# Reordering the output products of a fused attention and spectral-mix kernel, and moving rows of y by engines

## The chip, the cores and the metric

The kernel runs on one core of a Trainium2 chip. The metric is device time in microseconds for one launch. Engines are named as in the profile: PE (TensorE products), PEld (its weight loads), DVE (VectorE), ACT (ScalarE), POOL (GpSimd) and SP (SyncE, which here only issues transfers).

## The reference

Eight batch rows of causal attention with decay (8 heads, 576 positions, 64 channels each) give x, of shape 8 x 576 x 512. Then x is mixed in frequency space and by a channel matrix:

```python
X = np.fft.rfft(x, axis=1)
Xr, Xi = real(X[:, :64]), imag(X[:, :64])
Yr = einsum('bmd,mde->bme', Xr, w_r) - einsum('bmd,mde->bme', Xi, w_i)
Yi = einsum('bmd,mde->bme', Xr, w_i) + einsum('bmd,mde->bme', Xi, w_r)
Y[:, :64] = Yr + 1j * Yi
y = np.fft.irfft(Y, n=576, axis=1)
u = x + y
out = u + np.maximum(u @ w_ch, 0.0)
```

The weights w_r and w_i are 64 modes of 512 x 512 each in f32, 134 MB together. The output has 9.4 MB.

## The kernel before

**The weight stream.** The weights are cut into 64 tiles. POOL issues their transfers (line 90), which turn f32 into bf16, into a ring of nine buffers with the tag "wb". `emit_modes(n)` multiplies tile n (line 147), and the last half of the tiles (32 to 63) are the second half of the channels, two modes each. DVE adds the result to what the first half left, and writes rows of y's spectrum, "YT", of 2 x modes (line 164). Attention runs beside the first part of this stream.

**z in place of u @ w_ch.** The kernel computes z = u @ w_ch as a second sum with the same shape as u. XW = x @ w_ch is made early (`emit_xw`, line 775), and the rows of y are kept in two forms: t = 0 the rows themselves, t = 1 the rows times w_ch. Both are written into `yy`. Then u and z are each an x part (a product with the identity) plus a y part (a product with the inverse basis, BIe or BIl), and the output is u + max(z, 0).

**Early, mid and late rows.** Half of the modes (YTe) are ready early. `emit_part` adds their y parts into x_all and XW (the "early sums", 36; lines 739, 809 and 810). With four calls of `emit_y` for the early rows themselves they make a list of 40, which a counter spreads over the tiles 48 to 62. The other modes come in two quarters. The mid quarter is made by `emit_mid` (lines 784 to 790), the late quarter needs the last tile, 63, and is made by `emit_late` (lines 843 to 852). `y_rows` (line 723) makes both forms for four batch rows at a time: products with w_ch into `plw` (line 726), transposes into `ply` (line 734). ACT and DVE copy the two results to a buffer `yl`, and `move_rows` (line 704) brings each 32-row piece to its place in `yy` by a transfer: the mid ones on SP, 16 in all, the late ones on POOL. For the first batch row the late pieces are written by ACT and DVE directly (lines 848 and 849).

**The output loop.** There are 20 jobs, five for each pair of batch rows: four of 256 output rows and one of 64 rows of each of the two. The list of types gives jobs 5 and 11 to ACT and POOL (relu at line 887, sum at line 888); the others go to DVE. `emit_x` puts the x parts of a job into two PSUM tiles, pu and pz, and `emit_out` adds the y parts, has ACT copy pu to SBUF (line 883), DVE form the output (line 890), and SP store it (line 900 for 256 rows, line 896 for the half jobs). All PSUM tiles of this stage (pu, pz, A of tile 63, pl of `emit_late`) share one tag with four buffers of two banks each. For job 0 the x parts are issued three times before tile 63.

All these products are 64 x 64 tiles of the array. `pieces` gives the halves: with t = 0 for u and t = 1 for z, a piece's row half is `(b + t + (k if sb == 4 else 0)) % 2`, its column half is k.

**Who sets the order.** The framework's planner orders the instructions of each engine by program order and by its own estimate of when each is ready, so the queue of an engine can differ from the program. `tc.keep_in_program_order` pins an instruction in its place. SP and POOL issue transfers in their queue's order.

Of the kernel before, what the change touches and what calls it, by code (L numbers as in the profile page):

```python
# [21 lines left out]
def kernel(  # L22
# [11 lines left out]
    nc = tc.nc  # L34
# [84 lines left out]
    def emit_modes(n):  # L119
        dc, g = tile_of(n)  # L120
        wb = wtiles.pop(n)
        nm = MG if n < NTH else M2
        if late["psM"] is None:
            z = late["psZ"].tile([128, 2, D], F32, tag="z", name="A")
            A = z[:, 0, 0 : NDC * nm * 2 * B].rearrange(
                "p (e m c) -> p e m c", e=NDC, m=nm
            )
        else:
            A = late["psM"].tile([128, NDC, nm, 2 * B], F32, tag="A", name="A")
        if n < NTH:  # L130
# [12 lines left out]
        for mi in range(nm):  # L143
            m = g * nm + mi
            for eb in range(NDC):
                for i, (w_of, x_of) in enumerate(terms):
                    nc.tensor.matmul(  # L147
                        A[:, eb, mi, :],
                        lhsT=w_of(mi, eb * 128),
                        rhs=x_of(m),  # L150
                        start=(i == 0),
                        stop=(i == len(terms) - 1),
                    )
# [534 lines left out]
    with ExitStack() as bctx:  # L688
# [12 lines left out]
        yy = bsb.tile([128, 2, B // 2, 2, D], BF16, name="yy")  # L701
        yls = [bsb.tile([128, 2, D], BF16, name=f"yl{i}") for i in range(2)]

        def move_rows(yl, i, q, skip, dma):
            for j in range(skip, 4):
                for t in range(2):
                    p0 = HM * ((j + t) % 2) + H2 * i
                    dma(
                        yy[p0 : p0 + H2, 1, 2 * q + j // 2, t, :],
                        yl[H2 * j : H2 * j + H2, t, :],  # L710
                    )

        yflat = yy[:, :, :, :, :].rearrange("p l b t e -> p (l b t e)")
        xTs = [
# [8 lines left out]
        def y_rows(yt, b0, ply, plw):  # L723
            cols = lambda eb: _strided(yt[:, eb, b0, 0:1], [[1, 128]])
            for eb in range(NDC):
                nc.tensor.matmul(
                    plw,
                    lhsT=cols(eb),
                    rhs=wch[:, eb, :],
                    start=(eb == 0),  # L730
                    stop=(eb == NDC - 1),
                )
            for eb in range(NDC):
                nc.tensor.transpose(
                    ply[:, eb * 128 : (eb + 1) * 128], cols(eb), ident_bf[:, :]
                )

        def add(p, lhsT, rhs, first):
# [4 lines left out]
        with ExitStack() as cctx:  # L743
# [40 lines left out]
            def emit_mid(q):  # L784
                pyw = psBig.tile([128, D], F32, tag="big", name="pyw")
                yp = psBig.tile([128, D], BF16, tag="big", name="yp")
                y_rows(YT2[:, 0], 4 * q, yp[:, :], pyw[:, :])
                nc.scalar.copy(yls[q][:, 1, :], pyw[:, :])
                nc.vector.tensor_copy(yls[q][:, 0, :], yp[:, :])
                move_rows(yls[q], 0, q, 0, nc.sync.dma_start)  # L790

            def emit_part(b, sb):
                pA = psBig.tile([128, D], F32, tag="big", name="pA")
# [24 lines left out]
            while nmode < NT - 1:  # L818
# [5 lines left out]
                    nx += 1  # L824
                if nmode > NT - GL:
                    assert nx == B
                    while done < min(len(parts), (nmode - NT + GL) * len(parts) // (GL - 2)):
                        a, sb = parts[done]
                        emit_y(a) if sb is None else emit_part(a, sb)
                        done += 1  # L830
                if 0 <= nmode - NT + GL // 2 - 1 < 2:
                    emit_mid(nmode - NT + GL // 2 - 1)
            assert done == len(parts)

        psZ = bctx.enter_context(
            tc.tile_pool(
                name="psZ", bufs=4, space=bass.MemoryType.PSUM, reuse_waits="tile"
            )
        )
        late["psM"], late["psZ"] = None, psZ  # L840


        def emit_late(q):
            pl = psZ.tile([128, 2, D], F32, tag="z", name="pl")
            ply, plw = pl[:, 1, 0 : D // 2].bitcast(BF16), pl[:, 0, :]
            y_rows(YT2[:, 1], 4 * q, ply, plw)
            if q == 0:
                nc.scalar.copy(yy[HM + H2 : 128, 1, 0, 1, :], plw[0:H2, :])
                nc.vector.tensor_copy(yy[H2:HM, 1, 0, 0, :], ply[0:H2, :])
            nc.vector.tensor_copy(yls[q][:, 0, :], ply)  # L850
            nc.scalar.copy(yls[q][:, 1, :], plw)
            move_rows(yls[q], 1, q, 1 - q, nc.gpsimd.dma_start)

        def pieces(job):
            b, sb, nb, _ = job
# [8 lines left out]
                            BIl[HS[half], c0 : c0 + HM]  # L864
                        )

        def emit_x(job, times=1):
            pu = psZ.tile([128, 2, D], F32, tag="z", name="pu")
            pz = psZ.tile([128, 2, D], F32, tag="z", name="pz")
            for _ in range(times):  # L870
                for t, i, o, hs, src, _ in pieces(job):
                    add((pu, pz)[t][o, i, :], ident_bf[hs, hs], src, True)
            return pu, pz

        def emit_out(job, ps, last):
            b, sb, nb, ty = job
            for t, i, o, hs, _, basis in pieces(job):
                add(ps[t][o, i, :], basis, yy[hs, 1, b // 2, t, :], False)
            pu, pz = (p[:, 0:nb, :] for p in ps)
            uo = wpool.tile([128, 2, 2, D], F32, tag="wb", name="uo")  # L880
            u_sb, o_sb = uo[:, 0, 0:nb, :], uo[:, 1, 0:nb, :]
            if ty != "D":
                nc.scalar.copy(u_sb, pu)  # L883
            if ty == "D":
                nc.vector.scalar_tensor_tensor(o_sb, pz, 0.0, pu, ALU.max, ALU.add)
            elif ty == "Q":
                nc.scalar.activation(o_sb, pz, ACT.Relu)
                nc.gpsimd.tensor_tensor(o_sb, o_sb, u_sb, ALU.add)
            else:
# [30 lines left out]
_INS = ['q', 'k', 'v', 'f', 'moe_w_r', 'moe_w_i', 'moe_w_ch']  # L920
_OUTS = [((8, 576, 512), 'float32')]
# [25 lines left out]
```

## Time and profile before

| | |
|---|---|
| median of 5 runs | 446.21 us (444.36 to 447.98) |
| profiled execution | 445.05 us, span 443.2 us |
| mean granted PE clock | 0.861 |
| busy share of the span | PE 82%, DVE 58%, ACT 51%, POOL 30% |
| DMA | 98.20 MB written, mean 222 GB/s; HBM read 163.73 MB |
| mid moves `yy<-yl` on SP | 16 x 32 KB, issued 373.4 to 384.0 us, 5.2 us to landing |
| late moves `yy<-yl` on POOL | 14 x 32 KB, issued 406.8 to 415.6 us, 2.3 us to landing |
| stores of 512 KB | 16, 3.3 us to landing |

Times are microseconds from the start of the span. A row of a group or of the timeline gives engine, line, operation, the tile written and the tiles read, shapes and count; what stands in brackets is the idle time of the engine before it and what ended it. The share of DMA is the mean over 16 engines. Line 739 is a helper that issues the products of the early sums and of the output loop, so these are told apart by their tiles (pA, pB against pu, pz). The ends of products are modelled: a new group of products started every 0.2 us can show 0.38 us for each.

### The profile page before, as it was taken

What the parts mean: (1) busy time and instruction counts of PE and PEld (TensorE: products, weight loads), DVE (VectorE), ACT (ScalarE), POOL (GpSimd) and SP (SyncE); (2) the same over time, 40 slices, a digit from 0 to 9 for tenths busy, and PEclk for the clock granted to TensorE, in tenths of its full rate; (3) what the DMA queues carried; (4) which work ended last, traced back from release to release, by engine and by line L of the source; (5) the groups of instructions that cost most, each with busy time, mean ns of one, the idle gap of its engine ahead of it and who ended that gap; (6) DMA issues with size and microseconds to landing.
All of it is one profiled execution on the core that took longest, in us unless ns stands there. A gap on an engine that the chain in (4) does not pass through costs nothing.

```text
span 443.2 us, 12213 instructions
## 1 busy us (share of the span) xinstructions
PE 361.9 (82%) x5251; PEld 245.9 (55%) x5269; DVE 257.7 (58%) x643; ACT 223.8 (51%) x336; POOL 134.1 (30%) x204
## 2 busy tenths in 40 slices
PE   2787799999887976877877886999999779887873
PEld 1454566776666665655655665666655435543331
DVE  5687778876565655665656676334325535443554
ACT  3688377774645436436446382243354323333663
POOL 7333332252323323233232211432322323102520
PEclk9997699997977757758669597799999988989998
DMA  8999999999999999999999999999999999991787
GB/s 184 231 235 251 223 235 238 233 221 222 236 212 235 238 209 236 210 238 236 210 237 211 211 212 217 215 211 212 211 211 211 211 211 211 224 189 35 268 328 287
DMA packets 51126, 98.20 MB, mean 222 GB/s; under 512 B 3808, under 2 KB 13280, under 8 KB 51072
## 3 DMA queue, kind: packets, MB, share of 16 engines
q0 software_dynamic: 46688, 86.39, 99.4%
q1 hardware_dynamic: 4304, 10.90, 7.0%
q8 instruction: 41, 0.67, 0.5%
q10 hardware_dynamic: 80, 0.13, 0.1%
q14 instruction: 13, 0.11, 0.1%
HBM read 163.73 MB, written 9.44 MB: 391 GB/s over the span
## 4 chain that ended last, share of the span: by engine, by line
PE 31%; DMA 30%; ACT 13%; DVE 8%; issue 5%; POOL 1%; ACTq 0%; DVEq 0%
DMA wb<-in_moe_w_i_dram 30%; ACT E L517 8%; PE pav L555 7%; PE ps L510 6%; PE A L147 6%; PE tp L458 5%; PE px L598 2%; DVE QTs L473 2%; PE vp L482 2%; ACT KT L471 2%; ACT uo L883 2%; PE pz L739 2%; DVE uo L890 2%; PE px L623 1%; DVE E L532 1%
## 5 line engine op out<-in xcount | busy, mean ns | idle before, releaser
L517 ACT ACTIVATE E<-ps 128x1024 bf16<-128x1024 f32 (+1 forms) x128 | 101.5, 854 | 24.1 <-PE ps L510 14.8
L147 PE MATMUL A<-XT,wb 128*128 128x16 bf16 x2048 | 73.0, 181 | 14.8 <-DMA wb<-in_moe_w_i_dram 9.9
L90 POOL DMA_DIRECT2D wb<-in_moe_w_r_dram x65 | 43.2, 665 | 133.8 <-PE A L147 35.8
L147 PEld LDWEIGHTS <-wb 128*128 128x128 bf16 x2048 | 65.8, 99 | 30.0 <-issue 13.0
L510 PE MATMUL ps<-QTs,KT 64*128 64x64 bf16 (+4 forms) x384 | 56.1, 316 | 17.9 <-ACT E L517 16.7
L90 POOL DMA_DIRECT2D wb<-in_moe_w_i_dram x65 | 43.1, 662 | 78.9 <-DMA wb<-in_moe_w_i_dram 38.8
L555 PE MATMUL pav<-va,E 128*128 128x65 bf16 (+1 forms) x1088 | 53.6, 206 | 4.4 <-DVE x_all L577 3.8
L555 PEld LDWEIGHTS <-E 128*128 128x128 bf16 (+1 forms) x1088 | 43.9, 112 | 20.2 <-issue 9.5
L532 DVE TENSOR_TENSOR E<-E,trimask 128x256 bf16<-128x256 bf16 (+2 forms) x128 | 37.2, 302 | 20.0 <-ACT E L517 19.6
L810 ACT CAST XW<-pB 128x512 bf16<-128x512 f32 x36 | 21.1, 586 | 38.2 <-PE pB L739 38.2
L475 ACT COPY VT<-tp 128x640 bf16<-128x640 bf16 (+1 forms) x32 | 23.2, 755 | 32.9 <-PE tp L458 32.8
L775 ACT CAST XW<-pxw 128x512 bf16<-128x512 f32 x36 | 20.6, 587 | 35.9 <-PE pxw L768 27.4
L510 PEld LDWEIGHTS <-KT 64*128 64x128 bf16 x384 | 19.0, 98 | 30.1 <-issue 20.7
L809 DVE CAST x_all<-pA 128x512 bf16<-128x512 f32 x36 | 24.9, 692 | 18.0 <-PE pA L739 15.6
L768 PE MATMUL pxw<-wch,yy 128*128 128x512 bf16 x133 | 33.8, 387 | 1.0 <-issue 0.3
L471 ACT COPY KT<-tp 128x640 bf16<-128x640 bf16 (+1 forms) x32 | 22.1, 755 | 22.5 <-PE tp L458 22.5
L473 DVE COPY QTs<-tp 128x640 bf16<-128x640 bf16 (+1 forms) x32 | 23.2, 768 | 14.0 <-PE tp L458 13.9
L577 DVE TENSOR_TENSOR x_all<-pav,rcp 128x384 bf16<-128x384 f32 x64 | 29.1, 455 | 0.8
L739 PEld LDWEIGHTS <-ident_bf 64*64 64x64 bf16 (+1 forms) x304 | 15.1, 112 | 23.6 <-issue 18.2
L890 DVE SCALAR_TENSOR_TENSOR uo<-pz,uo 128x1024 f32<-128x1024 f32 (+1 forms) x18 | 19.4, 1103 | 12.9 <-ACT uo L883 10.8
L566 DVE RECIPROCAL rcp<-pav 128x6 f32<-128x6 f32 x64 | 12.1, 190 | 22.5 <-PE pav L555 21.8
L164 DVE TENSOR_TENSOR YTe<-A,Yacc 128x128 bf16<-128x128 f32 x16 | 5.9, 368 | 30.7 <-PE A L147 30.6
(127 smaller groups left out, 616.4 us busy)
## 6 DMA issues: line engine op xcount, KB each, us to landing
wb<-in_moe_w_r_dram POOLq DMA_DIRECT2D x63, 512.0 KB, 16.4
wb<-in_moe_w_i_dram POOLq DMA_DIRECT2D x63, 512.0 KB, 17.5
stv<-in_v_dram POOLq DMA_DIRECT2D x15, 576.0 KB, 15.1
out_dram<-uo SPq DMA_DIRECT2D x16, 512.0 KB, 3.3
stk<-in_k_dram POOLq DMA_DIRECT2D x16, 288.0 KB, 15.1
stq<-in_q_dram POOLq DMA_DIRECT2D x16, 288.0 KB, 15.1
out_dram<-uo SPq DMA_DIRECT2D x7, 128.0 KB, 3.7
stv<-in_v_dram SPq DMA_DIRECT2D x1, 576.0 KB, 4.6
```

Source lines behind the costliest of these rows:

```text
L90: tc.keep_in_program_order(nc.gpsimd.dma_start(dst, src))
L147: nc.tensor.matmul(A[:, eb, mi, :], lhsT=w_of(mi, eb * 128), rhs=x_of(m), start=(i == 0), stop=(i == len(terms) - 1),)
L471: nc.scalar.copy(rows(KTs[pr % 2][:, :, 0:S]), tv)
L473: nc.vector.tensor_copy(rows(QT[pr][:, :, :]), tv)
L510: nc.tensor.matmul(ps[:, b, o : o + n], lhsT=KTs[pr % 2][bs, h, jb * 128 : (jb + 1) * 128], rhs=QT[pr][bs, h, jb * 128 + c0 : jb * 128 + c ...
L517: nc.scalar.activation(E[:, :, piece * 512 : piece * 512 + w], ps[:, :, 0:w], ACT.Exp, scale=scale,)
L532: nc.vector.tensor_tensor(dg, dg, tr, ALU.mult)
L555: nc.tensor.matmul(pav[64 * half : 64 * half + w, slot, :], lhsT=E[:, b, c : c + (w - 1) * st + 1 : st], rhs=va[:, jb, b, :], start=(n == ...
L577: nc.vector.tensor_tensor(xo, pi, ri, ALU.mult)
L768: nc.tensor.matmul(pxw[:, :], lhsT=xT[:, eb, i * 128 : (i + 1) * 128], rhs=wch[:, eb, :], start=(eb == 0), stop=(eb == NDC - 1),)
L809: nc.vector.tensor_copy(xs, pA[:, :])
L890: nc.vector.scalar_tensor_tensor(o_sb, pz, 0.0, u_sb, ALU.max, ALU.add)
```

## The change

- `emit_mid` writes its 32-row pieces straight from PSUM to `yy` by DVE (t = 0) and ACT (t = 1), four each per call, in place of one copy each and eight transfers on SP.
- `y_rows` issues the transposes ahead of the products with w_ch.
- The counter of the early sums leaves two of the 40, both sums, to be issued behind tile 62; the x parts of job 0 are issued twice ahead of tile 63.
- The PSUM pool of the output stage has two tags, u and z, of two buffers each. A of tile 63 and plw take u, ply takes z.
- `emit_late` keeps only the sums and the direct copies. The copies to `yl` and the moves on POOL are in `emit_moves`, which for the first four batch rows is issued behind job 0's copy of u; the ACT copy in it is pinned.
- In the output loop the x and y products of z of job n are interleaved with those of u of job n + 1; the copy of u of job n + 1 is issued ahead of the output of job n.

```diff
-            z = late["psZ"].tile([128, 2, D], F32, tag="z", name="A")
+            z = late["psZ"].tile([128, 2, D], F32, tag="u", name="A")
...
-        def move_rows(yl, i, q, skip, dma):
-            for j in range(skip, 4):
-                for t in range(2):
-                    p0 = HM * ((j + t) % 2) + H2 * i
-                    dma(
-                        yy[p0 : p0 + H2, 1, 2 * q + j // 2, t, :],
-                        yl[H2 * j : H2 * j + H2, t, :],
-                    )
+        def row_slot(q, j, t, i):
+            p0 = HM * ((j + t) % 2) + H2 * i
+            return yy[p0 : p0 + H2, 1, 2 * q + j // 2, t, :]
...
             cols = lambda eb: _strided(yt[:, eb, b0, 0:1], [[1, 128]])
+            for eb in range(NDC):
+                nc.tensor.transpose(
+                    ply[:, eb * 128 : (eb + 1) * 128], cols(eb), ident_bf[:, :]
+                )
             for eb in range(NDC):
                 nc.tensor.matmul(
...
-            for eb in range(NDC):
-                nc.tensor.transpose(
-                    ply[:, eb * 128 : (eb + 1) * 128], cols(eb), ident_bf[:, :]
                 )
...
                 y_rows(YT2[:, 0], 4 * q, yp[:, :], pyw[:, :])
-                nc.scalar.copy(yls[q][:, 1, :], pyw[:, :])
-                nc.vector.tensor_copy(yls[q][:, 0, :], yp[:, :])
-                move_rows(yls[q], 0, q, 0, nc.sync.dma_start)
+                for j in range(4):
+                    rows = slice(H2 * j, H2 * j + H2)
+                    nc.vector.tensor_copy(row_slot(q, j, 0, 0), yp[rows, :])
+                    nc.scalar.copy(row_slot(q, j, 1, 0), pyw[rows, :])
...
-                    while done < min(len(parts), (nmode - NT + GL) * len(parts) // (GL - 2)):
+                    while done < (nmode - NT + GL) * (len(parts) - 2) // (GL - 2):
...
-                name="psZ", bufs=4, space=bass.MemoryType.PSUM, reuse_waits="tile"
+                name="psZ", bufs=2, space=bass.MemoryType.PSUM, reuse_waits="tile"
...
         def emit_late(q):
-            pl = psZ.tile([128, 2, D], F32, tag="z", name="pl")
-            ply, plw = pl[:, 1, 0 : D // 2].bitcast(BF16), pl[:, 0, :]
+            ply = psZ.tile([128, 2, D], F32, tag="z", name="ply")
+            plw = psZ.tile([128, 2, D], F32, tag="u", name="plw")[:, 0, :]
+            ply = ply[:, 0, 0 : D // 2].bitcast(BF16)
             y_rows(YT2[:, 1], 4 * q, ply, plw)
             if q == 0:
-                nc.scalar.copy(yy[HM + H2 : 128, 1, 0, 1, :], plw[0:H2, :])
-                nc.vector.tensor_copy(yy[H2:HM, 1, 0, 0, :], ply[0:H2, :])
-            nc.vector.tensor_copy(yls[q][:, 0, :], ply)
-            nc.scalar.copy(yls[q][:, 1, :], plw)
-            move_rows(yls[q], 1, q, 1 - q, nc.gpsimd.dma_start)
+                nc.vector.tensor_copy(row_slot(0, 0, 0, 1), ply[0:H2, :])
+                nc.scalar.copy(row_slot(0, 0, 1, 1), plw[0:H2, :])
+            return ply, plw
+
+        def emit_moves(q, pl):
+            nc.vector.tensor_copy(yls[q][:, 0, :], pl[0])
+            tc.keep_in_program_order(nc.scalar.copy(yls[q][:, 1, :], pl[1]))
+            for j in range(1 - q, 4):
+                for t in range(2):
+                    nc.gpsimd.dma_start(
+                        row_slot(q, j, t, 1), yls[q][H2 * j : H2 * j + H2, t, :]
+                    )
...
+        def start(job):
+            return tuple(
+                psZ.tile([128, 2, D], F32, tag=tag, name="p" + tag) for tag in "uz"
+            )
+
+        def terms(job, ps, t, what):
+            b, _, nb, _ = job
+            rows = [[] for _ in range(2 * nb)]
+            for tt, i, o, hs, src, basis in pieces(job):
+                if tt != t:
+                    continue
+                p = ps[t][o, i, :]
+                rows[2 * i].append((p, ident_bf[hs, hs], src, True))
+                rows[2 * i + 1].append((p, basis, yy[hs, 1, b // 2, t, :], False))
+            return [r for k, r in enumerate(rows) if "xy"[k % 2] in what]
+
+        def run(*lists):
+            for k in range(max(len(l) for l in lists)):
+                for l in lists:
+                    for a in l[k] if k < len(l) else ():
+                        add(*a)
+
+        def emit_u(job, ps):
+            uo = wpool.tile([128, 2, 2, D], F32, tag="wb", name="uo")
+            nc.scalar.copy(uo[:, 0, 0 : job[2], :], ps[0][:, 0 : job[2], :])
+            return uo
...
-        ps0 = emit_x(jobs[0], 3)
+        ps = start(jobs[0])
+        for _ in range(2):
+            run(terms(jobs[0], ps, 0, "x"), terms(jobs[0], ps, 1, "x"))
         emit_modes(nmode)
-        emit_late(0)
+        pl = emit_late(0)
+        run(terms(jobs[0], ps, 0, "y"), terms(jobs[0], ps, 1, "y"))
+        uo = emit_u(jobs[0], ps)
+        emit_moves(0, pl)
         for n, job in enumerate(jobs):
-            emit_out(job, emit_x(job) if n else ps0, n == len(jobs) - 1)
+            last = n == len(jobs) - 1
+            zs = terms(job, ps, 1, "xy") if n else []
+            us = []
+            if not last:
+                nxt = start(jobs[n + 1])
+                us = terms(jobs[n + 1], nxt, 0, "xy")
+            run(zs, us)
+            if not last:
+                uo_n = emit_u(jobs[n + 1], nxt)
+            emit_o(job, ps, uo, last)
+            if not last:
+                ps, uo = nxt, uo_n
             if n == 2:
-                emit_late(1)
+                emit_moves(1, emit_late(1))
```

More of the change, by code (lines that the diff above doesn't have):

```diff
@@ L731, in y_rows @@
                     stop=(eb == NDC - 1),
-                )
-            for eb in range(NDC):
-                nc.tensor.transpose(
-                    ply[:, eb * 128 : (eb + 1) * 128], cols(eb), ident_bf[:, :]
                 )
@@ L832 @@
                     emit_mid(nmode - NT + GL // 2 - 1)
-            assert done == len(parts)
+            for a, sb in parts[done:]:
+                emit_part(a, sb)
         psZ = bctx.enter_context(
             tc.tile_pool(
-                name="psZ", bufs=4, space=bass.MemoryType.PSUM, reuse_waits="tile"
+                name="psZ", bufs=2, space=bass.MemoryType.PSUM, reuse_waits="tile"
             )
@@ L865, in pieces, with emit_o @@
                         )
[L867 to L875, printed above, removed]
+        def start(job):
[21 more added lines that the diff above has]
+            return uo
+        def emit_o(job, ps, uo, last):
             b, sb, nb, ty = job
[L877 to L880, printed above, removed]
+            pz = ps[1][:, 0:nb, :]
             u_sb, o_sb = uo[:, 0, 0:nb, :], uo[:, 1, 0:nb, :]
[L882 to L886, printed above, removed]
+            if ty == "Q":
                 nc.scalar.activation(o_sb, pz, ACT.Relu)
```

## The prediction

> **What bounds the kernel now.** I read the chain that ended last first, then two-microsecond windows from 372 us on, then the timeline of the output part. The chain, by line and then in order of time:
>
> ```profile
> by line: DMA wb<-in_moe_w_i_dram 47.3%; ACT uo L883 9.7%; PE pz L739 9.1%; DVE uo L890 9.0%; issue 5.8%; DMA yy<-yl 3.7%; POOL yy L708 2.9%; PE pu L739 2.2%; PE pl L726 1.1%; ACT yl L851 0.8%; ACT yy L848 0.8%; ACT uo L887 0.7%; PE A L147 0
> ...
> 387.39 14.92 DMA wb<-in_moe_w_i_dram
> ...
> 427.44 1.23 DVE uo L890
> 428.67 0.04 issue
> 428.71 0.40 PE pz L739 x2
> ```
>
> Up to 402.3 us the chain is nothing but the weight stream. After that it is a zigzag: ACT copies pu, DVE makes the output, and only then may the next pz products start. Two stages, two bounds. The windows (busy us of PE, PEld, DVE, ACT, POOL; then granted clock, DMA share, GB/s) say how full each is:
>
> ```profile
> 376.00:378.00 2.00, 1.95 (x34) 1.15 (x30) 1.12 (x3) 1.34 (x3) 0.71 (x1) 1.00 1.12 215
> 378.00:380.00 2.00, 2.00 (x34) 1.15 (x30) 1.16 (x3) 0.53 (x2) 0.56 (x1) 1.00 1.13 225
> 380.00:382.00 2.00, 1.91 (x31) 1.20 (x29) 1.12 (x2) 1.27 (x3) 0.23 (x1) 1.00 1.15 231
> 386.00:388.00 2.00, 0.84 (x30) 0.83 (x30) 0.00 (x0) 0.00 (x0) 0.53 (x1) 0.97 1.13 218
> 388.00:390.00 2.00, 2.00 (x13) 0.89 (x12) 0.83 (x2) 0.00 (x0) 0.00 (x0) 0.50 1.14 218
> ...
> 428.00:430.00 2.00, 1.09 (x11) 0.40 (x10) 1.79 (x2) 1.06 (x2) 0.77 (x1) 1.00 0.24 92
> 430.00:432.00 2.00, 1.92 (x27) 1.32 (x27) 0.69 (x1) 0.91 (x2) 0.00 (x0) 1.00 1.01 401
> 434.00:436.00 2.00, 1.93 (x27) 0.75 (x17) 0.97 (x2) 1.41 (x2) 0.00 (x0) 1.00 1.02 396
> ```
>
> The DMA engines are full (share above 1) to 396 us. In the output part they change between full, at about 400 GB/s, and nearly empty: stores come late. The output loop in the timeline:
>
> ```profile
> 407.25 0.62 PE L739 MATMUL pz<-yy,BIl 64*64 64x512 bf16 x4
> 407.71 2.36 DVE L890 SCALAR_TENSOR_TENSOR uo<-pz,uo 128x1024 f32<-128x1024 f32 x2 [1.61 <-ACT uo L883]
> 417.14 2.36 POOL L888 TENSOR_TENSOR uo<-uo 128x1024 f32<-128x1024 f32 x1 [0.99 <-ACT uo L887]
> 419.53 3.44 SPq L900 DMA_DIRECT2D out_dram<-uo  x4
> 430.00 0.69 DVE L890 SCALAR_TENSOR_TENSOR uo<-pz,uo 128x512 f32<-128x512 f32 x1 [0.22 <-ACT uo L883]
> 438.05 0.69 DVE L890 SCALAR_TENSOR_TENSOR uo<-pz,uo 128x512 f32<-128x512 f32 x1 [0.17 <-ACT uo L883]
> ```
>
> Five jobs (one pair of batch rows) end with a half job at 414.7, about 422.5, 430.0 and 438.05 us on DVE: 23.3 us for the last three groups of five, 7.76 us each. No engine fills that time: DVE needs 4 x 1.23 + 0.69 = 5.6 us of it and ACT 4 x 1.02 + 0.59 = 4.7 us.
>
> **The change, part by part.**
>
> *Mid rows of y.* Removed: two ACT casts (0.586 us), two DVE copies (0.425) and 16 SP transfers of 32 KB (SP issues each in about 0.59 us; landing 5.2). Added: eight ACT casts of 32 x 512 at 0.574 us, by the row L848, and eight DVE copies at 0.413, by L849. Net ACT +3.4 us and DVE +2.5 us. They fall between 372 and 380 us, where both are at most two thirds busy, and the sums behind them can queue in six PSUM buffers; PE then waits 1.9 us for weights at 385.2 anyway. I cost them at nothing; if that cover is gone, 1.2 us (DVE) to 1.7 us (ACT) each time. On SP nothing stands behind the 16 transfers before the first store. What is gained is DMA time. While the 16 moves are under way the windows show 211, 215, 225, 231, 224, 228, 218 and 218 GB/s in place of 211: 82 x 2 us = 164 KB more, while 524 KB were moved. So 360 KB of weights were pushed back, 1.7 us at 211 GB/s. The lower end is 0, if the stream is held by its HBM reads, which the moves do not use.
>
> *Two early sums behind tile 62, x sums of job 0 twice, not three times.* PE reaches tile 62 two sums (2 x 0.86 us) sooner and waits there for the same weights (they end the wait at 397.35). Behind it: tile done at 398.27; two sums 1.72; their PSUM must be emptied before the output tiles take those banks, 0.7 (an L809 cast); 16 x products, 4 groups of four x 0.215 = 0.9; the first 16 products of tile 63, 0.56. That makes 402.1 us, against 402.36 where the last weights release the last 14 products. So it just fits. If the weights come 1.7 us sooner it fits by the same sliver, since tile 62 shifts too; but there is no slack. I keep 1.0 of the 1.7 us. Ends: -1.7, and +2.4 us if PE runs this stretch at half clock. The window at 388 shows that clock (0.50) after a wait of 1.9 us, and the wait before tile 62 grows from 1.3 us to about 3.
>
> *Late rows.* ply and plw get a tile each, transposes first. In one tile DVE's copy L849 waited for ACT's L848 (404.63 to 405.24). Now DVE is done by about 404.4 and ACT by 405.3; job 0's u sums end at once, and its copy starts at 405.3 where it started at 406.67. Job 0's store gains 1.3 us. But the ACT copy yl is held behind that copy: it ends about 406.9, where it ended at 406.77, and the POOL queue's second transfer waits for it: issue 407.4, landed 2.3 us later at 409.7. Waiting for that: z of job 2 and u of job 3 in PE's queue. Then 0.86 us of products, and job 2 leaves DVE at about 411.8; before, 411.6. Job 1 loses its early start too: plw takes the slot of A, so u of job 1 waits for the copy of u of job 0 (406.3). Job 4 comes out level with before; I cost the whole at 0 (ends -1, +1).
>
> *The output loop.* u of job n+1 goes out with z of job n. The copy of u then lies one turn ahead of DVE, and both run side by side. What is left per turn is the slower of PE and DVE. PE: 64 x 64 products run four at once when they use both row halves and both column halves, a group each 0.215 us (24 x products of job 0 in 1.42 us). u of a batch row uses one half of the rows, z the other. So z of (b, first) with u of (b, second) makes 4 groups, 0.86 us. But z of b with u of b+1 falls on the same half: 8 groups of two, 1.72 us. The two turns with a half job make 6 groups, 1.29 us each. PE in five turns: 28 groups, 6.0 us. Taking the slower of PE and DVE (1.24) in each turn: 1.24 + 1.72 + 1.24 + 1.29 + 1.29 = 6.8 us, against 7.76. Three groups of five: 2.9 us; the last evacuation ends at 435.8, not 438.7.
>
> Here a rule speaks against the change. By the Trainium skill ("TensorE: Matmul & The Clock Gate", Part 3, "The mechanism"), a weight load overlaps running products only if its row group differs. The 20 same-half groups of five turns would then show loads of 0.106 us: one each is +2.1 us, both +4.2, and the loop gets slower. The first row of the last fence speaks otherwise: four products of pz on one half take 0.62 us, two groups started 0.21 us apart, each product 0.38 long. I take the trace.
>
> *What is late next: the stores.* They leave in order on SP. Job 5's output is added on POOL (2.36 us), behind ACT's relu, which now comes behind the copy of u of job 6; I leave its store where it is, 419.5, and the stores of jobs 6 and 7 wait behind it. From 420.5 the rest, 15 jobs or 7.1 MB, takes 17.7 us at 400 GB/s: 438.2. Job 11, the other job with POOL, leaves a hole of about 1.1 us: 439.3. Before, DMA was busy to 441.5. Gain 2.2 us, not 2.9. The skill ("DMA: Bandwidth & Descriptors", "Specifications") gives about 358 GB/s of HBM for a core: 19.8 us, 441.4 with the hole, and next to no gain. The windows of the stores show 401 and 396, so I take 400.
>
> **Sum.** -1.0 (weights) + 0 (start) - 2.2 (output) = -3.2 us. The profiled execution took 445.05 us (span 443.2), the median of the five is 446.21, 1.2 us above it. By the profiled one 441.9; against the median, which I forecast, 443.0 us.
>
> **The rivals.**
>
> *B: the gain is swallowed.* Either the planner, which reorders PE's queue (in the trace x products of job 1 stand ahead of job 0's y products), puts u far ahead of z, so that everything runs two at once: 36 groups x 0.215 = 7.7 us per five jobs, the old 7.76. Or the stores wait for job 5 and job 11 longer than I think. Then only part of the weights' 1.0 us is left, or the two sums behind tile 62 eat it: 445.5 us. For it: 0.25 us of room before tile 63, and DMA engines that are 75% full already (9.4 MB in the 31.6 us from 409.9 us on are 298 GB/s of 400). Against it: z and u stand interleaved in the queue, and each has its own two buffers.
>
> *C: PE becomes the bound and slower than the zigzag.* Place: the 20 same-half groups per five turns. If the weight loads show there, between the two prices above, say 0.16 us a group, five turns take 6.0 + 3.2 = 9.2 us. Over 3.7 groups of five that is 1.44 x 3.7 = +5.3 us; less the weights' 1.0: 450.5 us. It decides from (7.76 - 6.0) / 20 = 0.09 us per group on. For it: the rule, and a PE that is busy nearly all the time. Against it: the row at 407.25, and a clock of 1.00 to 438 us.
>
> **How the numbers follow.** A, as summed: 0.65, with its own range 440 to 445 (weights 0 to 1.7, start +1 to -1, output 1 to 4). B: 0.20. C: 0.15. About 0.5% (2.2 us) is what a measurement of this kernel can tell from no change; the border is 444.0. Of A 0.53 lie below it and 0.12 above; of B 0.02 and 0.18; of C 0.14 are slower, and half clock before tile 63 with no gain in the loop adds 0.02 out of B and A. So faster 0.55, same 0.29, slower 0.16. The range runs from 439.0 (everything at its good end, but for the stores) to 449.0, which takes in half clock before tile 63 (+2.4 over the median) and the milder half of C.
>
> **What would show it.** Right: the weights' last products start about 1 us sooner than 402.36; half jobs on DVE follow each other in under 7 us; DMA near 400 GB/s from 421 us with one hole; ACT copies of u no longer end DVE's idle time, PE pz does. Wrong: clock 0.5 between 396 and 401 us and the last tile of weights waiting for PE; same-half groups over 0.3 us apart; pz products in runs without pu between them; the GB/s row of the moves' windows unchanged without the moves.

## The result, and the profile after

The changed kernel takes 442.82 us in the median of 21 runs (441.46 to 445.07); the kernel before takes 446.33 us in 40 runs beside it. The ratio is 0.992, with an interval of 0.9901 to 0.994. The prediction said 443.0. The profiled execution of the changed kernel took 442.82 us, span 441.0.

The chain of the changed kernel from 366 us on, by line, and three of its pieces:

```profile
by line: DMA wb<-in_moe_w_i_dram 51.2%; PE pz L734 8.9%; issue 6.9%; PE pu L734 6.5%; POOL yy L855 5.9%; DVE uo L907 5.0%; PE pA L734 4.1%; PE pB L734 3.8%; PE A L147 3.4%; ACT uo L896 3.3%; DMA yy<-yl 1.9%; DVEq L975 1.8%; PE plw L725 1.0%
...
371.16 21.33 DMA wb<-in_moe_w_i_dram
...
401.57 0.91 PE A L147 x32
...
430.91 1.24 DVE uo L907
```

The zigzag is gone from most of the output part. Of the chain from 366 us on, ACT's copies of u have 3.3% and DVE's outputs 5.0%, where they have 9.2% and 8.6% of the same stretch before, and products of pz and pu follow each other. New in it are products of pA and pB from 392 us to tile 63: PE, not DMA, ends the weight part. Behind tile 63 the chain runs over POOL's moves of the late rows (404.9 to 413.1 us, with 3.05 us between the moves of the first four batch rows and those of the others). The windows (busy us of PE, PEld, DVE, ACT, POOL; clock, DMA share, GB/s):

```profile
376.00:378.00 2.00, 1.95 (x41) 1.43 (x41) 1.96 (x5) 1.39 (x3) 0.71 (x1) 1.00 1.12 211
378.00:380.00 2.00, 1.84 (x18) 0.79 (x14) 1.55 (x4) 1.95 (x5) 0.56 (x1) 1.00 1.11 209
380.00:382.00 2.00, 1.14 (x34) 1.01 (x36) 0.41 (x2) 0.54 (x2) 0.54 (x1) 1.00 1.13 214
...
394.00:396.00 2.00, 2.00 (x12) 0.86 (x10) 0.69 (x1) 0.58 (x1) 0.00 (x0) 0.50 1.04 194
396.00:398.00 2.00, 2.00 (x21) 0.83 (x18) 1.02 (x2) 0.70 (x2) 0.00 (x0) 0.67 0.64 120
...
416.00:418.00 2.00, 1.50 (x22) 0.62 (x21) 1.55 (x2) 1.78 (x3) 1.96 (x1) 1.00 0.48 151
...
426.00:428.00 2.00, 1.98 (x19) 0.71 (x14) 1.86 (x3) 0.94 (x2) 0.97 (x1) 1.00 0.27 100
...
430.00:432.00 2.00, 1.89 (x26) 1.07 (x23) 1.63 (x2) 1.18 (x3) 0.00 (x0) 1.00 1.01 381
...
434.00:436.00 2.00, 0.01 (x1) 0.00 (x0) 1.56 (x2) 0.00 (x0) 0.00 (x0) 1.00 1.00 406
```

The bulge of the GB/s row (231 before) is gone. DVE (376 us) and ACT (378 us) are nearly full where they copy the mid rows. From 394 to about 397 us PE runs at half clock. The stores have two holes, at 416 and 426 us, and are full from 428 us to the end.

For the comparison of all runs I divided each profile at one point: the end of DVE's sum of tile 63 (the last YT row). Before it lies the weight part, behind it the output part up to the end of the span. The row of the kernel before, then that of the changed kernel:

```profile
402.91 0.37 DVE L164 TENSOR_TENSOR YT<-A,Yacc 128x128 bf16<-128x128 f32 x1 [4.24 <-PE A L147]
```

```profile
402.50 0.36 DVE L164 TENSOR_TENSOR YT<-A,Yacc 128x128 bf16<-128x128 f32 x1 [1.19 <-PE A L147]
```

For the kernel before, 402.91 + 0.37 = 403.28 and 443.2 - 403.28 = 39.92. The ratios are of runs taken side by side, so they are not quite the quotients of the medians. The last three columns are from one profile of each kernel.

| kernel | median us | ratio to before (95%) | sum of tile 63 ends | first output row on DVE, after that | output part |
|---|---|---|---|---|---|
| before | 446.33 | | 403.28 | 4.43 | 39.92 |
| changed | 442.82 | 0.992 (0.9901-0.994) | 402.86 | 3.00 | 38.14 |
| e1_mid | 445.12 | 0.9949 (0.9927-0.9972) | 401.77 | 5.16 | 40.93 |
| e2_sums | 446.24 | 0.9999 (0.9976-1.0021) | 404.31 | 4.44 | 39.99 |
| e3_loop | 443.75 | 0.9943 (0.9917-0.9969) | 403.75 | 3.00 | 38.15 |
| e4_apart | 441.99 | 0.9885 (0.9842-0.9927) | 402.30 | 3.01 | 37.50 |
| e5_qpool | 443.17 | 0.9925 (0.9898-0.9952) | 402.36 | 3.00 | 38.94 |
| e6_noq | 441.14 | 0.9871 (0.983-0.9912) | 402.14 | 3.00 | 35.86 |
| e7_apart_noq | 439.80 | 0.9844 (0.9802-0.9886) | 402.38 | 2.99 | 35.62 |
| e8_sumsoff | 442.61 | 0.9905 (0.987-0.9941) | 401.94 | 3.34 | 38.66 |
| e9_ufirst | 441.62 | 0.99 (0.9867-0.9933) | 401.16 | 4.03 | 38.84 |
| e10_late | 444.48 | 0.997 (0.9949-0.9991) | 402.65 | 4.06 | 39.85 |
| e11_before_noq | 446.21 | 1.0004 (0.9973-1.0034) | 403.61 | 5.50 | 41.29 |
| e12_tfirst | 446.37 | 1.0004 (0.9979-1.0029) | 402.90 | 5.49 | 41.00 |

### The profile page after: what moved, and what is told of

It reads as the page before. It is cut to its first block, busy times and chain, and to the rows that moved or that the text cites. A ratio compares the mean times of both kernels' runs of the same rounds, so it can differ in the third digit from the quotient of the medians.

```text
span 441.0 us, 12172 instructions
## 1 busy us (share of the span) xinstructions
PE 361.0 (82%) x5243; PEld 246.9 (56%) x5261; DVE 259.4 (59%) x649; ACT 227.4 (52%) x342; POOL 133.5 (30%) x204
## 4 chain that ended last, share of the span: by engine, by line
PE 32%; DMA 29%; ACT 11%; DVE 9%; issue 6%; POOL 1%; DVEq 0%; ACTq 0%; POOLq 0%
DMA wb<-in_moe_w_i_dram 26%; ACT E L517 7%; PE pav L555 7%; PE ps L510 6%; PE A L147 5%; PE tp L458 5%; DMA stv<-in_v_dram 3%; PE px L598 2%; DVE QTs L473 2%; PE vp L482 2%; ACT KT L471 2%; PE pz L734 2%; DVE XT L612 1%; DVE E L532 1%; PE pu L734 1%
## 5 line engine op out<-in xcount | busy, mean ns | idle before, releaser
L147 PE MATMUL A<-XT,wb 128*128 128x16 bf16 x2048 | 72.1, 181 | 16.6 <-DMA wb<-in_moe_w_i_dram 12.0
L734 PEld LDWEIGHTS <-ident_bf 64*64 64x64 bf16 (+1 forms) x296 | 16.8, 111 | 18.4 <-issue 12.2
L566 DVE RECIPROCAL rcp<-pav 128x6 f32<-128x6 f32 x64 | 12.1, 190 | 22.7 <-PE pav L555 21.9
```

Of the source, the lines that this page charges most:

```text
L147: nc.tensor.matmul(A[:, eb, mi, :], lhsT=w_of(mi, eb * 128), rhs=x_of(m), start=(i == 0), stop=(i == len(terms) - 1),)
L734: nc.tensor.matmul(p, lhsT=lhsT, rhs=rhs, start=first, stop=not first, skip_group_check=True)
```

## The experiments

**Each part alone.** First the mid rows, on the kernel before (`row_slot` is the changed kernel's):

```diff
-                nc.scalar.copy(yls[q][:, 1, :], pyw[:, :])
-                nc.vector.tensor_copy(yls[q][:, 0, :], yp[:, :])
-                move_rows(yls[q], 0, q, 0, nc.sync.dma_start)
+                for j in range(4):
+                    rows = slice(H2 * j, H2 * j + H2)
+                    nc.vector.tensor_copy(row_slot(q, j, 0, 0), yp[rows, :])
+                    nc.scalar.copy(row_slot(q, j, 1, 0), pyw[rows, :])
```

> The kernel before with the mid rows of y copied by DVE and ACT to their places, in place of 16 transfers on SP; all else as before. Theory (the moves pushed back weights in full DMA engines): the last products of tile 63 start 1.0 to 1.7 us sooner than 402.36 us, and the time falls by as much, to 444.6 to 445.3 us against 446.3. Rival (the stream is held elsewhere, or PE is late for the last tile): tile 63 ends where it did and the time stays within 0.3 us. Rival (the 3.4 us more of ACT work and 2.5 us of DVE stall the early sums): time up by 1 us or more, with ACT ending PE's idle time between 372 and 380 us.

Measured: 445.12 us, 0.3% to 0.7% below before. The last products of tile 63 in the kernel before:

```profile
402.36 0.51 PE L147 MATMUL A<-XT,wb 128*128 128x16 bf16 x14 [1.01 <-DMA wb<-in_moe_w_i_dram]
```

Of e1_mid, the added copies of one `emit_mid`, the same products, and the window that had 231 GB/s before:

```profile
374.93 2.34 ACT L795 CAST yy<-pyw 32x512 bf16<-32x512 f32 x4 [0.44 <-PE pyw L730]
...
400.86 0.51 PE L147 MATMUL A<-XT,wb 128*128 128x16 bf16 x14 [0.82 <-DMA wb<-in_moe_w_i_dram]
...
380.00:382.00 2.00, 2.00 (x45) 1.63 (x45) 1.52 (x4) 1.78 (x4) 0.54 (x1) 0.85 1.12 210
```

The last products still wait for weights, and start at 400.86, not 402.36: 1.5 us sooner, in the predicted span. The eight ACT casts take 2 x 2.34 us, but PE waits for neither ACT nor DVE between 370 and 386 us. In this profile the clock is 0.85 at its highest from 366 us on, so PE is slower there than in the others, and its output part cannot be compared with theirs. In the changed kernel, at 1.00, PE's only waits in that stretch are for weights too. So full DMA engines carried the moves at the weights' expense, and the copies were free. The rivals fall.

Second, the early sums, on the kernel before:

```diff
-                    while done < min(len(parts), (nmode - NT + GL) * len(parts) // (GL - 2)):
+                    while done < (nmode - NT + GL) * (len(parts) - 2) // (GL - 2):
...
-        ps0 = emit_x(jobs[0], 3)
+        ps0 = emit_x(jobs[0], 2)
```

> The kernel before with two early sums left behind tile 62 and the x sums of job 0 issued twice, not three times; all else as before. Theory (it just fits in the wait for the last weights): no change, within 0.4 us, tile 63 not later than 402.9 us. Rival (the longer wait before a late tile drops the PE clock, and the two sums then run at half clock): PEclk of 0.5 somewhere in 394 to 401 us, tile 63 late for its weights by 1 us or more, time up by 1 to 2.4 us.

Measured: no change of the time, as the theory said, but its profile shows what the rival said: tile 63 ended 1.0 us late (404.31), and the clock had been 0.59 from 386 to 392 us and 0.77 from 392 to 396. Nothing in that profile pays for it (the output part is that of before, and the execution took 446.16 us against 445.05). The time of the other executions does not show it; the runs below give a possible reason.

Third, the late rows and the output loop alone:

```diff
                 y_rows(YT2[:, 0], 4 * q, yp[:, :], pyw[:, :])
-                for j in range(4):
-                    rows = slice(H2 * j, H2 * j + H2)
-                    nc.vector.tensor_copy(row_slot(q, j, 0, 0), yp[rows, :])
-                    nc.scalar.copy(row_slot(q, j, 1, 0), pyw[rows, :])
+                nc.scalar.copy(yls[q][:, 1, :], pyw[:, :])
+                nc.vector.tensor_copy(yls[q][:, 0, :], yp[:, :])
+                for j in range(4):
+                    for t in range(2):
+                        nc.sync.dma_start(
+                            row_slot(q, j, t, 0), yls[q][H2 * j : H2 * j + H2, t, :]
+                        )
...
-                    while done < (nmode - NT + GL) * (len(parts) - 2) // (GL - 2):
+                    while done < min(len(parts), (nmode - NT + GL) * len(parts) // (GL - 2)):
...
-        for _ in range(2):
+        for _ in range(3):
             run(terms(jobs[0], ps, 0, "x"), terms(jobs[0], ps, 1, "x"))
```

> The changed kernel with the mid rows back on SP transfers and the early sums and the three x sums back as before: only the late rows and the output loop are changed. Theory (additive, as in the sum): 2.2 us below the kernel before, 444.1 us, and half jobs on DVE about 7.2 us apart as in the changed kernel. Rival (all of the gain lies in the output part): 3.5 us below, 442.8 us, no difference to the changed kernel. Rival (most of it lies in the weights): within 1 us of before.

Measured: 0.6% below before (0.3 to 0.8), that is 2.6 us, near the predicted 2.2. Its half jobs on DVE are 7.2 us apart and its output part is 38.15 us, the changed kernel's 38.14: the loop's gain does not depend on the other edits. With 0.5% for the mid rows and 0.0% for the sums, the parts add to 1.1%; the whole has 0.8% (0.6 to 1.0). The intervals allow that.

**The sums again, with the weights sooner.** The changed kernel with the last two hunks of e3_loop only:

> The changed kernel with the early sums all ahead of tile 62 and the x sums of job 0 three times, as before; mid rows by engines, late rows and output loop stay changed. Theory (once the weights come 1.5 us sooner the two sums behind tile 62 make PE late for tile 63, in the trace by 1.1 us against the run with the mid rows alone): 0.5 to 1 us below the changed kernel, 442.0 us. Rival (they cost nothing, as they did in the kernel before): the same 442.8 us. Rival (they help, by taking sums away from the stretch before): 443.5 us or more.

Measured: 442.61 us, the same as the changed kernel, as the first rival said. In its profile tile 63 ended 0.9 us sooner (401.94) and the output part was 0.5 us longer. The last products of tile 63 in the changed kernel, in e8_sumsoff, and in e9_ufirst, a run told below that has the changed kernel's program up to here:

```profile
401.50 0.96 PE L147 MATMUL A<-XT,wb 128*128 128x16 bf16 x32
```

```profile
401.02 0.51 PE L147 MATMUL A<-XT,wb 128*128 128x16 bf16 x14 [0.85 <-DMA wb<-in_moe_w_i_dram]
```

```profile
400.25 0.51 PE L147 MATMUL A<-XT,wb 128*128 128x16 bf16 x14 [0.72 <-DMA wb<-in_moe_w_i_dram]
```

In the first PE is late and finds all its weights there; in the other two it waits for them. So the two sums alone do not make PE late: with a clock of 1.00 from 386 to 400 us they fit (e9_ufirst, whose tile 63 is the earliest of all, 401.16). Nor does the half clock alone: in e8_sumsoff and e10_late it lies at 393 to 396 us, and PE still waits 0.85 and 1.03 us for the last weights. In the six profiles that have both, the sums behind tile 62 and a half clock between 387 and 402 us (changed, e2, e4 to e7), PE is late.

The window behind tile 63 (columns as above) of e8_sumsoff:

```profile
404.00:406.00 2.00, 2.00 (x16) 1.00 (x17) 0.72 (x1) 1.50 (x2) 1.51 (x3) 0.50 0.13 33
```

The same window of e12_tfirst, a run told below:

```profile
404.00:406.00 2.00, 2.00 (x9) 0.40 (x9) 0.09 (x1) 0.57 (x1) 0.00 (x0) 0.50 0.00 0
```

And of the kernel before:

```profile
404.00:406.00 2.00, 1.89 (x18) 0.83 (x19) 0.73 (x2) 0.57 (x1) 0.00 (x0) 1.00 0.00 0
```

Half clock behind tile 63 makes the output part start slower. From the end of tile 63's sum to the end of job 4 on DVE it is 12.08 us before and 13.13 in e12_tfirst, 11.08 in the changed kernel and 12.01 in e8_sumsoff. In the profiles with the two sums behind tile 62, all but that of e9_ufirst, the clock is back at 1.00 by 404 us; without them it is half behind tile 63 in e1, e8, e10, e11 and e12, but not in the kernel before and in e3_loop. So with the two sums a half clock costs about 1 us ahead of tile 63, and with or without them about 1 us behind it. This may be why the sums change no time. One profile of each kernel does not tell how often each happens, so that balance is not shown. That the kernel before can be cold there too follows from e11_before_noq, which has the same program up to the output.

**What the order of the products is worth.** The changed kernel with z and u in blocks:

```diff
-            run(zs, us)
+            run(zs)
+            run(us)
```

> The changed kernel, but z products of job n are issued ahead of the u products of job n + 1, not interleaved with them; copies and outputs as in the changed kernel. Theory (PE's order counts: products of one row half run two at a time, 36 groups of 0.215 us in five turns in place of 28): PE at 7.7 us per five jobs, half jobs on DVE 7.7 us apart, the gain of the loop gone: 445 us. Rival (what counts is that the copy of u lies one turn ahead of DVE; the stores are the bound from job 5 on): within 0.5 us of the changed kernel, 442.8 us. Rival (the planner's queue keeps them mixed anyway): the queue shows pu and pz alternating and the time is unchanged.

Measured: 441.99 us (six executions, all below the changed kernel's median), and half jobs on DVE 6.6 us apart (412.97 to 432.80 for three groups of five), closer than the 7.2 of the changed kernel. My theory falls. The queue, read from the compiled kernels (z, u: x products; Z, U: y products), and the timeline of e4_apart:

```
changed    zzuuZZUUzzuuZZUUzzuuZZUU
e4_apart   zzZZzzZZuuUUuuUUzzZZzzZZ
```

```profile
421.68 0.38 PE L734 MATMUL pu<-x_all,ident_bf 64*64 64x512 bf16 x1
...
421.94 0.37 PE L734 MATMUL pz<-x_all,ident_bf 64*64 64x512 bf16 x1
...
422.11 0.38 PE L734 MATMUL pu<-x_all,ident_bf 64*64 64x512 bf16 x1
...
422.16 0.40 PE L734 MATMUL pz<-yy,BIl 64*64 64x512 bf16 x2
422.33 0.41 PE L734 MATMUL pu<-yy,BIl 64*64 64x512 bf16 x2
422.38 0.38 PE L734 MATMUL pz<-x_all,ident_bf 64*64 64x512 bf16 x1
```

Eight z products stand ahead of eight u products in the queue, yet groups of both start in turn, 0.05 us apart. So the queue's order does not make PE take one block behind the other, and the loss did not come. Of the rivals the first is the nearest, but the time is 0.8 us below the changed kernel's, where it allowed 0.5; the third falls, since the queue does hold blocks.

> The changed kernel with the u products of job n + 1 issued ahead of the z products of job n, each in one block. Theory (z first helps because DVE, which waits for z, is the engine that paces the loop, and u has a turn of slack): slower than z first (442.0 us) and than the mixed order (442.8 us), 443.3 us or more, half jobs on DVE 7.5 us apart or more. Rival (what helps is the block, which lets the two row halves of the array run past each other, whichever comes first): as z first, 442.0 us.

The same with the two lines exchanged: 441.62 us, half jobs 6.6 us apart. The theory (z first) falls. In both block orders DVE's half jobs follow closer than in the mixed order, whichever block comes first. Why is not shown, and z first and u first cannot be told apart with six executions each.

**The two jobs on ACT and POOL.** On the changed kernel, first their stores on POOL's queue, then no such jobs:

```diff
-                nc.sync.dma_start(
+                (nc.gpsimd if ty == "Q" else nc.sync).dma_start(
```

> The changed kernel with the stores of jobs 5 and 11 (the two that are added on POOL) issued from POOL's queue, so that the stores of jobs 6, 7, 12 and 13 on SP don't stand behind them. Theory (the holes of the stores come from waiting in order on SP, as the prediction's last step has it): DMA is no longer empty at 416 to 418 and 426 to 428 us, 1 to 2 us less: 441 us. Rival (in the trace of the changed kernel job 6 leaves DVE at 417.7 us and job 5's store is issued at 417.99, so that DVE, held by ACT's relu and copies, is as late as POOL): within 0.5 us of the changed kernel.

```diff
-        jobs = [(*j, ty) for j, ty in zip(jobs, "NNNNNQNNNNNQNNNNNNNN")]
+        jobs = [(*j, ty) for j, ty in zip(jobs, "N" * 20)]
```

> The changed kernel with jobs 5 and 11 given to DVE like the others: no relu on ACT, no sum on POOL. Theory (the holes in the stores come from these two jobs as such: relu ahead of copies on ACT, 2.36 us of POOL, SP in order): DMA stays near 400 GB/s from 415 us on, the last store leaves 1 to 2 us sooner: 441 to 442 us. Rival (DVE is then the bound, 2.4 us more of it over the loop): no gain, or up to 1 us slower, half jobs on DVE over 7.2 us apart.

Moving the stores changes nothing (443.17 us; the DMA share at 416 to 418 us is still only 0.27). Giving the jobs to DVE takes 1.7 us off (441.14; five of its six executions lie below the fastest of the changed kernel's 21), and DMA is full from 418 us on, about as the theory said. DVE's rows in the changed kernel, then in e6_noq:

```profile
416.45 2.36 DVE L907 SCALAR_TENSOR_TENSOR uo<-pz,uo 128x1024 f32<-128x1024 f32 x2 [2.51 <-ACT uo L896]
...
433.74 1.82 DVE L907 SCALAR_TENSOR_TENSOR uo<-pz,uo 128x1024 f32<-128x1024 f32 x2 [0.40 <-PE pz L734]
```

```profile
413.82 1.22 DVE L907 SCALAR_TENSOR_TENSOR uo<-pz,uo 128x1024 f32<-128x1024 f32 x1 [0.60 <-ACT uo L896]
415.33 2.43 DVE L907 SCALAR_TENSOR_TENSOR uo<-pz,uo 128x1024 f32<-128x1024 f32 x2 [0.29 <-PE pz L734]
...
431.69 1.82 DVE L907 SCALAR_TENSOR_TENSOR uo<-pz,uo 128x1024 f32<-128x1024 f32 x2 [0.40 <-PE pz L734]
```

With the relu in ACT's queue, DVE waits 2.51 us for ACT's next copy; without it, 0.60 for ACT and 0.29 for PE. So the holes in the stores come from the way of these two jobs over ACT and POOL, which holds DVE up as well, not from SP's order. e6_noq takes relu and POOL's sum away together and does not part them.

> The kernel before with all 20 jobs on DVE, no relu on ACT and no sum on POOL. Theory (in the zigzag of ACT, DVE and PE of the kernel before, two jobs on ACT and POOL relieve it; only the new loop makes them a burden): no gain, or up to 1 us slower. Rival (the two jobs cost by themselves, by their late stores): 1.5 us below before, as between the changed kernel and the one without them.

On the kernel before, the same edit gives no change (ratio 1.0004), as the theory said. The two jobs are a burden only once the loop is pipelined.

> Both: z products issued ahead of the u products of the next job, and all jobs on DVE. Theory (z first brings DVE's work 0.4 us sooner per turn, as in the run with z ahead of u, and the stores have no more holes): below that run by 1 us or more, 441.0 us or less, with DMA full from 413 us to the end. Rival (the stores are full already from 419 us on there, and DVE gets 2.4 us more): 442.0 us or above.

Both edits, blocks and all jobs on DVE: 439.80 us, the lowest median of all, 1.6% below before (1.1 to 2.0), as the theory said. From e6_noq it is not clear of the spread of six executions each: the medians differ by 1.3 us, but the profiles have the same span, 438.0 us. Half jobs are 6.3 us apart. Two windows of 4 us:

```profile
420.00:424.00 4.00, 3.95 (x47) 2.00 (x44) 3.73 (x4) 3.11 (x4) 0.00 (x0) 1.00 0.99 362
424.00:428.00 4.00, 4.00 (x51) 2.34 (x53) 3.11 (x4) 2.66 (x4) 0.00 (x0) 1.00 1.03 410
```

DMA is full, and PE busy, in both; the DMA share is 0.92 from 416 us and full from 418, not from 413 as the theory had it. The loop's last DVE row ends 1.7 us sooner than in e6_noq (431.85 against 433.51), and the output part is only 0.24 us shorter: the stores are the bound there.

**The late rows.** On the kernel before:

```diff
-            pl = psZ.tile([128, 2, D], F32, tag="z", name="pl")
-            ply, plw = pl[:, 1, 0 : D // 2].bitcast(BF16), pl[:, 0, :]
+            ply = psZ.tile([128, 2, D], F32, tag="z", name="ply")
+            plw = psZ.tile([128, 2, D], F32, tag="z", name="plw")[:, 0, :]
+            ply = ply[:, 0, 0 : D // 2].bitcast(BF16)
```

and in `y_rows` the transposes ahead of the products.

> The kernel before with only the late rows changed: ply and plw in a tile each, transposes ahead of the products with w_ch; copies, moves and output loop as before. Theory (the start of the output part gains nothing by job 4, as in the sum): within 0.4 us of before, though DVE's copy of ply no longer waits for ACT's. Rival (a part of the loop's 2.7 us is the start): 0.6 us or more below before.

Measured: 0.3% below before (0.1 to 0.5), while the output part of its profile is as long as before (39.85). But the two profiles differ in the clock behind tile 63, and the next run makes up for that.

> The kernel before with one edit: y_rows issues the transposes ahead of the products with w_ch, for the early, mid and late rows; ply and plw stay in one tile. The run with this and separate tiles was 0.3% faster (0.1 to 0.5), though its output part, counted from the end of tile 63, was as long as before. Theory (the edit's effect lies in the early and mid rows, by the place of the short transposes in the early sums): the same 0.3%, about 445.0 us. Rival (it comes with the separate tiles, in the first microseconds of the output part): no change, 446.3 us. Rival (what was seen there is the spread of the weights' end from run to run, 402.7 to 404.3 us in the profiles without the engine moves): no change, and the end of tile 63's sum on DVE between 402.7 and 404.3 us.

The order in `y_rows` alone: no change. Its profile has half clock behind tile 63, and so has that of e10_late, so these two can be compared. The window and the first output row of e10_late, then that row of e12_tfirst (its window is shown above):

```profile
404.00:406.00 2.00, 2.00 (x13) 0.89 (x15) 0.02 (x1) 1.40 (x3) 1.28 (x3) 0.50 0.06 15
...
406.71 1.23 DVE L891 SCALAR_TENSOR_TENSOR uo<-pz,uo 128x1024 f32<-128x1024 f32 x1 [2.69 <-ACT uo L884]
```

```profile
408.39 2.36 DVE L890 SCALAR_TENSOR_TENSOR uo<-pz,uo 128x1024 f32<-128x1024 f32 x2 [1.61 <-ACT uo L883]
```

From the end of tile 63's sum to the end of job 4 on DVE, in us, by the clock behind tile 63:

| clock | start as before | with ply and plw in a tile each | with that and the new loop |
|---|---|---|---|
| 1.00 at 404 us | 12.08 (before), 12.09 (e2) | no run | 11.08 (changed), 11.09 (e3) |
| 0.50 at 404 us | 13.14 (e11), 13.13 (e12) | 12.01 (e10) | 12.01 (e8) |

At equal clock the separate tiles save 1.1 us of the start (and of the output part, 39.85 against 41.00), the new loop adds nothing to that, and the half clock costs about 1 us. So the 0.3% of e10_late (1.3 us) is about what its edit saves in the start: its theory falls, and the rival that names the separate tiles holds. The spread of the weights' end (402.65 to 404.31 in the six profiles without the engine moves) is as large, so the time alone would not have told. Where the saving comes from shows in DVE's copy of the late rows, of the kernel before and of the changed kernel:

```profile
405.24 0.41 DVE L849 COPY yy<-pl 32x512 bf16<-32x512 bf16 x1 [1.96 <-ACT yy L848]
```

```profile
403.36 0.41 DVE L846 COPY yy<-ply 32x512 bf16<-32x512 bf16 x1 [0.49 <-PE ply L721]
```

In one tile the copy waits for ACT's; in its own it does not.

## Why the prediction was right, point by point

*The sum* was -3.2 us, and -3.5 was measured in the medians. In the profiles it is -2.2 (443.2 to 441.0), because the profiled execution of before (445.05) lies 1.3 us under its median and that of the changed kernel on it. So the hit of 443.0 is in part luck: from the profile that it started from, the prediction had 441.9, and 442.82 was measured. Two of its terms also missed by about 1 us each and cancelled.

*Weights, -1.0:* right. In the pair of profiles it is only -0.42 (403.28 to 402.86), since the half clock at 394 us made PE late, the end that the prediction priced. Over all profiles, the sum of tile 63 ends at 403.42 in the mean without the engine moves (before, e2, e3, e10, e11, e12) and at 402.11 with them (changed, e1, e4 to e9): -1.3 us; the two groups overlap. By e1_mid's time the term is 1.2 us (medians) to 2.3 us (ratio). The mid copies cost nothing, as said.

*The sums behind tile 62, "just fits":* right at full clock (e9_ufirst). At half clock PE is late for tile 63 by about 1 us, which the prediction saw as a risk. It did not see that a half clock behind tile 63 costs as much, so that the sums need not show in the time.

*The start, 0:* mis-sized, within its ends of -1 and +1. From the end of tile 63's sum to the end of job 4 on DVE: 12.1 us before (415.36 - 403.28), 11.1 after (413.94 - 402.86). It is -1.0, and at equal clock it comes with the separate tiles (e10 against e12), not with the loop's order. The prediction gave job 0 its 1.3 us and took them back by job 2, which was to wait for a move that POOL issues at 407.4. In the changed kernel POOL issued its moves of the first four rows from 404.92 to 408.07 us, and job 2 left DVE at 410.51, 7.65 us behind tile 63's sum, where the prediction had 411.8, 8.5 us behind it.

*The output loop, -2.9:* mis-sized the other way. From job 4 to job 19 on DVE: 23.4 us before, 21.6 after (413.94 to 435.56), -1.8: 7.2 us per five jobs, not 6.8. The term left out is ACT's relu in two turns, which holds up ACT's next copy; e6_noq, without it, gives 6.8 (413.21 to 433.51). But e4_apart and e9_ufirst, with the relu and in blocks, give 6.6, so the order counts as well, and the count of groups behind the 6.8 is not confirmed. The statement that ACT copies would no longer end DVE's waits was wrong. Before, changed, and e6_noq (in all, times, longest):

```profile
DVE uo L890 <- ACT uo L883: 10.8, 10, 2.6
```

```profile
DVE uo L907 <- ACT uo L896: 9.3, 7, 2.5
```

```profile
DVE uo L907 <- ACT uo L896: 4.4, 5, 1.6
```

So giving the two jobs to DVE takes away about half of what was left. Start and loop together are -2.8, where -2.9 was forecast: the two misses cancel.

*The stores take some back:* right. DVE ends 2.8 us sooner after tile 63 (35.46 to 32.70), the span 1.8. The prediction had 2.9 and 2.2. The holes stand at the two jobs where it put them, but not for SP's order (e5). The stores run at 377 to 406 GB/s from 428 us on, near the 400 that it took from the trace and above the 358 that it set aside.

*Rival B:* the planner kept the order as written, so its mechanism did not occur; e4 and e9 show that even blocks would not have cost time. *Rival C:* not seen. Rows on one half of the array, in the changed kernel:

```profile
414.48 0.35 PEld L734 LDWEIGHTS <-BIl 64*64 64x64 bf16 x4
...
414.69 0.41 PE L734 MATMUL pz<-yy,BIl 64*64 64x512 bf16 x2
414.91 0.41 PE L734 MATMUL pu<-yy,BIl 64*64 64x512 bf16 x2
```

They are 0.22 us apart, and the weight loads run beside products of the same half. The trace, not the rule as the prediction cites it, was the right guide.

## What to carry to other kernels

When a stage's chain is a zigzag of two evacuating engines, issue the other engine's input one turn ahead and give each its own buffers; then ask which engine got the odd jobs of the old balance (here ACT's relu), since a split that was neutral in the zigzag costs 1.7 us in the pipeline. Small on-chip moves are not free while the DMA engines are full: without 0.5 MB of them the weights came about 1.3 us sooner here. And before two profiles are compared near a wait, see that their clock is the same there: the gain of e10_late was hidden by 3.4 us of half clock.

## What the hardware showed beyond that

Products on different row halves of the array passed each other here. In e4_apart eight products of one half stand in PE's queue ahead of eight of the other, and the second eight start 0.17 us behind the first (422.11 against 421.94), where one after the other would be 0.86 (four groups of two, 0.215 us each). The Trainium skill ("TensorE: Matmul & The Clock Gate", Part 3, "The mechanism") has products start and end in strict order of the program; the starts in this trace of 64 x 64 tiles do not agree (the ends are modelled). So a count of groups by the queue's order, as in the theory of e4_apart, does not hold.

The half clock comes in stretches of one length. Added up over windows of half a microsecond, each stretch of 0.50 is 3.4 us long (388 to 391 us before, 394 to 397 us in the changed kernel), or twice that (e2_sums from 387 us, e11_before_noq from 400 us). Where it falls is not told by the wait ahead of it. It came 0.8 to 1.9 us behind waits of PE for weights of 2.9 us (changed), 2.1 us (e8_sumsoff, e12_tfirst) and 1.2 us (e4_apart), but none came within 6 us of a wait of 2.3 us in e10_late (to 386.8 us) and of one of 1.9 us in e3_loop (to 382.4 us). What sets its place stays open.
